# Attention and feed-forward on one core: unread products fill TensorE from its first microseconds

## The chip, the cores and the metric

The kernel runs on one core of a Trainium2 chip. The metric is the device time of one execution in microseconds (us); smaller is better.

## What is computed

Causal attention over 8 batches of 8 heads, 576 tokens and 64 features a head, with 16 extra keys and values ("beacon") that every token sees; its output goes through a feed-forward layer of 512 to 2048 to 512 with a squared rectifier. Cut to what matters:

```python
k_all = concatenate([beacon_k, k], axis=2); v_all = concatenate([beacon_v, v], axis=2)
scores = q @ k_all.T / sqrt(64)          # later tokens masked
a = exp(scores - max); a /= a.sum(-1)
x = (a @ v_all) as [4608 tokens, 512]
out = maximum(x @ w_in, 0) ** 2 @ w_out  # float32
```

## The kernel before, in words

A batch's heads are handled in four pairs. For each pair, q and k are turned so that features lie on partitions: batches 0 to 2 by transposes on TensorE (L635 where VectorE or ScalarE has first regrouped the data to full width, L638 straight from the cast data), later ones by DMA. VectorE and ScalarE copy the results to `kT` and `qT` (L437 and L439, which also hold all casts). Scores come from products that use 64 of the 128 rows of the array (L764), ScalarE takes the exponential into `pt` (L781), VectorE masks it (L799, L803), TensorE multiplies with the values `vb` (L819), VectorE normalises (L834, L835), and TensorE (batch 0, L883) or a DMA turns the result into `xT`. Batch 0 does this in two phases, tokens up to 240 first, so that the feed-forward part can start early. The feed-forward part goes by chunks of 512 tokens: products with `w_in` (L947), rectifier (L964, L966), square (L973), products with `w_out` (L987), copy and store.

Loads of q and k of the first batches, of some values and of the weights are issued by GpSimd (L599, L484, L908, L917), the others by SyncE. GpSimd also casts most values and makes the identity `ident` from a tile that VectorE has zeroed (L409).

The order of the instructions on every engine is made when the kernel is built. `Order.run` (L155) plays through the operations with a duration, a priority and dependences for each, an own model of the DMA rings, and pools of PSUM banks; each engine's queue is then emitted in the order found. That plan knows nothing of the chip's real times, and the queue of each engine is fixed by it.

The planner has a filler: where TensorE is free in the plan's time between the two values of `FILL` (L136) and no operation is ready, it puts in a pair of products of the identity with itself into the PSUM bank that has been free the longest. Nobody reads these. Their form follows the operation before: 64 rows (L533), 64 columns (L535) or the full array (L537). `mode` stands for that form; where it changes, the plan adds `DRAIN` to the duration. A filler counts 0.11 us in the plan. It takes the place in the queue that the plan gives it, however late the queue is on the chip.

Of the kernel before, what the change touches and what calls it, by code (L numbers as in the profile page):

```python
# [129 lines left out]
class Order:  # L130
# [2 lines left out]

    LAT = {"PE": 0.2, "ACT": 0.15, "DVE": 0.12, "POOL": 0.15, "SP": 0.1, "-": 0.0}
    DRAIN = 0.096
    FILL = (10.0, 22.0)  # L136
    filler = None
    START = {"PE": 0.0, "ACT": 0.0, "DVE": 1.5, "POOL": 0.5, "SP": 0.0, "-": 0.0}

# [15 lines left out]
    def run(self):  # L155
# [19 lines left out]
        full = False  # L175
# [5 lines left out]
        now = 0.0  # L181
        mode = None
        while events:
            now = events[0][0]
# [6 lines left out]
            full = full and rings.packets("SP") > rings.ROOM  # L191
            while events and events[0][0] <= now + 1e-9:
                _, _, kind, op = heapq.heappop(events)
# [17 lines left out]
            while again:  # L211
                again = False
                for e in engines:
                    if free[e] > now + 1e-9 or (e == "SP" and full):
                        continue
                    best = None
# [4 lines left out]
                    for op in avail[e]:  # L221
# [21 lines left out]
                        if best is None or op.prio < best.prio:  # L243
                            best = op
                    if best is None:
                        best = fallback
                    if best is None and e == "PE" and self.filler is not None and self.FILL[0] <= now < self.FILL[1]:
                        spot = self.pools["ps"].oldest()
                        if spot is not None:
                            best = self.filler(spot, mode or "full")  # L250
                            self.ops.append(best)
                            avail[e].append(best)
                    if best is None:
                        continue
                    op = best
# [13 lines left out]
                    if e == "PE":  # L269
                        dur += self.DRAIN * (mode not in (None, op.mode))  # L270
                        mode = op.mode
# [6 lines left out]
                    if op.dma:  # L278
                        rings.put(e, op, now + (0.75 + 0.6 * op.dma if e == "POOL" else 0.9))
                        under[e] += 1  # L280
                        full = full or (e == "SP" and rings.packets(e) > rings.ROOM)
# [29 lines left out]
def kernel(  # L311
# [11 lines left out]
    nc = tc.nc  # L323
# [17 lines left out]
    def sb(name, shape, dt):  # L341
        return pool.tile(shape, dt, name=name)
# [26 lines left out]
    ident = sb("ident", [128, 128], BF16)  # L369
    warm = sb("warm", [128, 8], FP32)  # L370
    xT = sb("xT", [128, NMC, RING], BF16)
# [4 lines left out]
    ps = psum.tile([128, 8, 512], FP32, name="ps")  # L376
# [25 lines left out]
    order.wait_for = wait_for  # L402
    add = order.add

    nc.vector.memset(warm, 0.0)
    for i in range(2):
        nc.vector.memset(kT[i][:, :, Nb + S:NT * 128], 0.0)
# [115 lines left out]
        deps += [o for p in range(HP * (b - 2), HP * (b - 1)) for o in qk_ops[p]]  # L523
        trans[b, x] = [add(f"tr{b}{x}", "SP", 3.8, emit, prio=prio, deps=deps, dma=3.4, margin=2.0)]

    def filler(spot, mode):


        def emit(e):
            for i in range(2):  # L530
                half = slice(64 * i, 64 * i + 64)
                if mode == "rows":
                    nc.tensor.matmul(ps[:, spot, 0:128], ident[0:64, :], ident[0:64, :], start=True, stop=True)  # L533
                elif mode == "columns":
                    nc.tensor.matmul(ps[half, spot, 0:128], ident[:, half], ident, start=True, stop=True)  # L535
                else:
                    nc.tensor.matmul(ps[:, spot, 0:128], ident, ident, start=True, stop=True)  # L537

        op = Op("fill", "PE", 0.11, emit, mode=mode)
        op.left, op.held = 0, None  # L540
        return op

# [600 lines left out]
```

## Time and profile before

| what | us |
|---|---|
| median of 3 runs | 339.43 |
| lowest and highest run | 338.14, 339.49 |
| profiled execution | 338.65 |
| its span, first to last instruction | 336.9 |
| TensorE busy in the span | 327.1 |

The profile is of one execution. Its span leaves out what lies around the instructions, 338.65 - 336.9 = 1.75 us. Times in the rows of the prediction count from the start of the span. PE is TensorE's products, PEld its weight loads, DVE VectorE, ACT ScalarE, POOL GpSimd, SP SyncE; a q behind the name is the engine's sequencer. A product's duration runs from its start to its modelled end, so neighbouring products overlap, and the time that one costs in a queue is the distance of the starts.

### The profile page before, as it was taken

Reading aid. Unit: us, or ns where it says so; the run is one execution under the profiler, and the core shown is the slowest. Engines: PE = TensorE matmul, PEld = TensorE weight load, DVE = VectorE, ACT = ScalarE, POOL = GpSimd, SP = SyncE. Lnnn points to the kernel's source line nnn. Section 1 sums busy time; section 2 is a strip of 40 time slices with the busy share of each in tenths; the row PEclk is TensorE's granted clock in tenths of the full one; section 3 lists DMA queues with packets and bytes.
Section 4 is the critical chain, followed back from the end, with each engine's and each line's share of the span. In section 5 each row is a group of like instructions: output and inputs, shape, how many; then the busy total and the mean of one; then the engine's idle time right before and its main releaser. Section 6 shows DMA issues by size and latency. Waiting matters only on the chain.

```text
span 336.9 us, 7692 instructions
## 1 busy us (share of the span) xinstructions
PE 327.1 (97%) x3172; PEld 184.2 (55%) x3172; DVE 160.5 (48%) x323; ACT 193.6 (57%) x300; POOL 86.8 (26%) x135
## 2 busy tenths in 40 slices
PE   3999999999999999999999999999999999999995
PEld 2778766545545555554468845545554544444444
DVE  6669977267604761475245632673246503301400
ACT  3887974597457647465656745755656226515611
POOL 7765911425122605140512351220000000000000
PEclk9999999999999999999999999999999999999999
DMA  9999999699959999799989996991310041011003
GB/s 167 196 207 210 206 203 207 147 247 179 221 104 223 241 199 176 185 208 228 206 121 257 242 210 138 209 196 32 104 62 2 14 120 63 0 62 64 0 17 110
DMA packets 138211, 50.38 MB, mean 150 GB/s; under 512 B 124176, under 2 KB 133264, under 8 KB 138176
## 3 DMA queue, kind: packets, MB, share of 16 engines
q1 hardware_dynamic: 128304, 40.42, 57.7%
q0 software_dynamic: 9520, 9.11, 16.3%
q8 instruction: 25, 0.41, 0.6%
q10 hardware_dynamic: 352, 0.36, 0.4%
q14 instruction: 10, 0.08, 0.1%
HBM read 37.22 MB, written 9.44 MB: 138 GB/s over the span
## 4 chain that ended last, share of the span: by engine, by line
PE 93%; DMA 2%; POOL 1%; DVE 1%; issue 1%; ACT 0%; POOLq 0%
PE ps L947 37%; PE ps L987 36%; PE ps L819 9%; PE ps L764 8%; DMA qk_area<-in_q_dram 2%; PE ps L635 1%; PE ps L1030 1%; POOL qk_area L599 1%; PE ps L883 1%; DVE g L966 0%; PE ps L537 0%; POOL vb L439 0%; PE ps L533 0%; POOL w_in L908 0%; DVE g L973 0%
## 5 line engine op out<-in xcount | busy, mean ns | idle before, releaser
L947 PE MATMUL ps<-xT,w_in 128*128 128x512 bf16 (+3 forms) x704 | 133.7, 340 | 0.2
L987 PE MATMUL ps<-w_out,g 128*128 128x512 bf16 x560 | 128.4, 379 | 0.0
L781 ACT ACTIVATE pt<-ps 128x1024 bf16<-128x1024 f32 (+3 forms) x128 | 102.9, 874 | 18.3 <-PE ps L764 18.1
L947 PEld LDWEIGHTS <-w_in 128*128 128x128 bf16 x704 | 65.9, 98 | 55.2 <-issue 3.9
L964 ACT ACTIVATE g<-ps 128x512 bf16<-128x512 f32 (+2 forms) x116 | 65.5, 568 | 39.1 <-PE ps L947 38.6
L987 PEld LDWEIGHTS <-g 128*128 128x128 bf16 x560 | 52.1, 98 | 61.1 <-issue 3.6
L973 DVE TENSOR_TENSOR g<-g 128x1024 bf16<-128x1024 bf16 (+2 forms) x80 | 52.1, 654 | 69.6 <-ACT g L964 69.4
L437 ACT COPY osb<-ps 128x512 f32<-128x512 f32 (+2 forms) x37 | 21.3, 576 | 68.8 <-PE ps L987 54.6
L439 POOL CAST qk_area<-stg 128x512 bf16<-128x512 f32 (+2 forms) x50 | 34.2, 688 | 67.5 <-DMA stg<-in_q_dram 41.0
L439 POOL CAST vb<-stg 128x512 bf16<-128x512 f32 (+1 forms) x39 | 26.1, 675 | 63.3 <-DMA stg<-in_v_dram 63.2
L799 DVE TENSOR_TENSOR pt<-pt,tri 128x1024 bf16<-128x1024 bf16 (+1 forms) x36 | 23.5, 654 | 34.2 <-ACT pt L781 34.2
L819 PEld LDWEIGHTS <-pt 128*128 128x128 bf16 (+1 forms) x960 | 34.2, 98 | 6.3 <-ACT pt L781 0.4
L966 DVE TENSOR_SCALAR g<-ps 128x512 bf16<-128x512 f32 (+2 forms) x44 | 26.8, 611 | 19.7 <-PE ps L947 19.4
L819 PE MATMUL ps<-vb,pt 128*128 128x65 bf16 (+1 forms) x960 | 35.6, 195 | 0.4 <-POOL vb L439 0.3
L764 PE MATMUL ps<-qT,kT 64*128 64x80 bf16 (+6 forms) x680 | 32.9, 235 | 0.0
L764 PEld LDWEIGHTS <-kT 64*128 64x128 bf16 x680 | 19.0, 96 | 16.8 <-issue 13.8
L835 DVE TENSOR_TENSOR xn<-ps,rcp 128x640 bf16<-128x640 f32 (+2 forms) x36 | 27.0, 750 | 1.8 <-DVE rcp L834 0.5
L834 DVE RECIPROCAL rcp<-ps 128x10 f32<-128x10 f32 (+2 forms) x36 | 7.5, 209 | 28.9 <-PE ps L819 28.9
L437 ACT COPY qT<-ps 128x576 bf16<-128x576 bf16 x12 | 7.6, 644 | 8.4 <-PE ps L635 7.4
L803 DVE TENSOR_TENSOR pt<-pt,tri 80x160 bf16<-80x160 bf16 x32 | 11.1, 347 | 0.0
L439 DVE COPY kT<-ps 128x576 bf16<-128x576 bf16 x12 | 8.9, 751 | 1.8 <-PE ps L638 1.2
L635 PE MATMUL ps<-ident,sparek 96*128 96x96 bf16 x18 | 1.5, 229 | 5.8 <-DVE sparek L439 5.8
(52 smaller groups left out, 80.4 us busy)
## 6 DMA issues: line engine op xcount, KB each, us to landing
out_dram<-osb SPq DMA_DIRECT2D x17, 512.0 KB, 3.6
stg<-in_v_dram SPq DMA_DIRECT2D x20, 256.0 KB, 5.1
stg<-in_q_dram SPq DMA_DIRECT2D x20, 256.0 KB, 5.5
stg<-in_k_dram SPq DMA_DIRECT2D x15, 256.0 KB, 4.3
w_in<-in_moe_w_in_dram POOLq DMA_DIRECT2D x4, 512.0 KB, 8.8
w_out<-in_moe_w_out_dram POOLq DMA_DIRECT2D x4, 512.0 KB, 11.6
stg<-in_v_dram SPq DMA_DIRECT2D x7, 224.0 KB, 4.5
qk_area<-in_k_dram POOLq DMA_DIRECT2D x4, 288.0 KB, 11.5
```

What stands on the lines that cost most here:

```text
L437: nc.scalar.copy(dst, src)
L439: eng[e].tensor_copy(dst, src)
L764: nc.tensor.matmul(st[:, hj, lo + col:lo + col + t1 - t0], kT[x.b % 2][hp, x.pr, 128 * c:128 * c + 128], qT[x.b % 2][hp, x.pr, t0:t1], sta ...
L781: nc.scalar.activation(pt[x.take_pt.held[0]][:, :, off:off + width], pair(box["qk"], k)[:, :, lo:lo + width], AF.Exp, bias=0.0, scale=scale)
L799: nc.vector.tensor_tensor(out=d, in0=d, in1=tri[:, m0:m0 + m, :][:, None].to_broadcast([128, 2, m, 128]), op=ALU.min)
L819: nc.tensor.matmul(a[:, hj, (t - tl[0]) * (D + 1):(t - tl[0] + 1) * (D + 1)], P[0:rr, hj, o:o + 128], vb[b % 2][0:rr, c, h, :], start=(c = ...
L835: nc.vector.tensor_tensor(out=xn[b % 2].rearrange("p t (h d) -> p h t d", d=D)[:, 2 * pr:2 * pr + 2, tl[0]:tl[0] + nt], in0=a[:, :, :, 0:D ...
L947: nc.tensor.matmul(h[:, lo - spans[0][0]:hi - spans[0][0]], w_in_sb[:, mc, ft * 128:(ft + 1) * 128], xT[:, mc, lo % RING:lo % RING + hi - lo],
L964: nc.scalar.activation(dst, h, AF.Relu, bias=0.0, scale=1.0)
L966: nc.vector.tensor_scalar(out=dst, in0=h, scalar1=0.0, scalar2=None, op0=ALU.max)
L973: nc.vector.tensor_tensor(out=d, in0=d, in1=d, op=ALU.mult)
L987: nc.tensor.matmul(o, G[:, fc, ts * 128:(ts + 1) * 128], w_out_sb[:, fc, :], start=(fc == 0), stop=(fc == NFT - 1))
```

## The change

The planner's fillers may come from 0.6 us of its time on, instead of 10.0. Up to 2.6 they are one product of 128x128 with 128x512 from a zeroed stretch of `xT`, called `hot`, into bank 7, and count 0.43 us. After that they are pairs of products of the identity, which count 0.22 us up to 6.0 and 0.11 us behind. The form with 64 rows is gone: after an operation of that form the filler is of the full array. After one of the 64-column form a pair still has that form, but the plan takes every filler as one of the full array, and adds `DRAIN` where the operation before had another form. VectorE zeroes `hot` as its first instruction.

```diff
-    FILL = (10.0, 22.0)
+    FILL = (0.6, 22.0)
...
-                            best = self.filler(spot, mode or "full")
+                            best = self.filler(spot, mode or "full", now)
...
+    hot = xT[:, 0, 0:512]
+    nc.vector.memset(hot, 0.0)
     nc.vector.memset(warm, 0.0)
...
-    def filler(spot, mode):
-
+    def filler(spot, mode, now):
+
+
+        mode = "columns" if mode == "columns" else "full"
+        if now < 2.6:
+            def emit(e):
+                nc.tensor.matmul(ps[:, 7, :], hot[:, 0:128], hot, start=True, stop=True)
+
+            op = Op("fill", "PE", 0.43, emit)
+            op.left, op.held = 0, None
+            return op
 
         def emit(e):
             for i in range(2):
                 half = slice(64 * i, 64 * i + 64)
-                if mode == "rows":
-                    nc.tensor.matmul(ps[:, spot, 0:128], ident[0:64, :], ident[0:64, :], start=True, stop=True)
-                elif mode == "columns":
+                if mode == "columns":
                     nc.tensor.matmul(ps[half, spot, 0:128], ident[:, half], ident, start=True, stop=True)
                 else:
                     nc.tensor.matmul(ps[:, spot, 0:128], ident, ident, start=True, stop=True)
 
-        op = Op("fill", "PE", 0.11, emit, mode=mode)
+        op = Op("fill", "PE", 0.22 if now < 6.0 else 0.11, emit, mode=mode)
```

## The prediction before the run

> **What bounds the kernel now.** I read the page first, then the instructions of TensorE in order of time, then the groups by shape, the waits and the single DMA issues. The page says who is the bound:
>
> ```profile
> span 336.9 us, 7692 instructions
> PE 327.1 (97%) x3172; PEld 184.2 (55%) x3172; DVE 160.5 (48%) x323; ACT 193.6 (57%) x300; POOL 86.8 (26%) x135
> PEclk9999999999999999999999999999999999999999
> ```
>
> TensorE is busy for all but 9.8 us of the span. So a change can win only at the start, where TensorE has nothing to do or is slow, or it must take work out of the queue behind. The clock row shows full speed from the first slice; the next rows show that it can't be trusted there. Start, duration, operation, count, and in brackets the idle time before:
>
> ```profile
> 5.80 0.66 PE L635 MATMUL ps<-ident,sparek 96*128 96x96 bf16 x6 [5.80 <-DVE sparek L439]
> ...
> 8.65 1.27 PE L638 MATMUL ps<-ident,qk_area 96*64 96x96 bf16 x24
> 9.86 0.84 PE L764 MATMUL ps<-qT,kT 64*128 64x240 bf16 x8
> 10.63 1.17 PE L638 MATMUL ps<-ident,qk_area 96*64 96x96 bf16 x24
> 11.73 1.53 PE L764 MATMUL ps<-qT,kT 64*128 64x240 bf16 x16
> 13.52 1.10 PE L819 MATMUL ps<-vb,pt 128*128 128x65 bf16 x12 [0.26 <-POOL vb L439]
> 14.75 0.38 PE L883 MATMUL ps<-ident,xn 112*128 112x112 bf16 x2
> 14.92 0.85 PE L537 MATMUL ps<-ident 128*128 128x128 bf16 x6
> 15.56 0.54 PE L819 MATMUL ps<-vb,pt 128*128 128x65 bf16 x6
> 15.91 0.62 PE L537 MATMUL ps<-ident 128*128 128x128 bf16 x4
> 16.32 0.40 PE L883 MATMUL ps<-ident,xn 112*128 112x112 bf16 x2
> 16.52 0.54 PE L819 MATMUL ps<-vb,pt 128*128 128x65 bf16 x6
> 16.99 0.53 PE L764 MATMUL ps<-qT,kT 64*128 64x336 bf16 x4
> 17.45 0.38 PE L883 MATMUL ps<-ident,xn 112*128 112x112 bf16 x2
> 17.76 0.38 PE L764 MATMUL ps<-qT,kT 64*128 64x208 bf16 x4
> 17.98 0.72 PE L533 MATMUL ps<-ident 64*128 64x128 bf16 x10
> 18.63 0.28 PE L883 MATMUL ps<-ident,xn 112*128 112x112 bf16 x2
> 18.85 0.35 PE L764 MATMUL ps<-qT,kT 64*128 64x336 bf16 x4
> 19.04 0.38 PE L533 MATMUL ps<-ident 64*128 64x128 bf16 x4
> 19.31 0.35 PE L764 MATMUL ps<-qT,kT 64*128 64x336 bf16 x4
> 19.59 0.99 PE L947 MATMUL ps<-xT,w_in 128*128 128x240 bf16 x8
> ```
>
> Compare like with like: two L883 take 0.38 to 0.40 us up to 17.45, and 0.28 at 18.63; four L764 of width 336 take 0.53 at 16.99 and 0.35 at 18.85. Six fillers of 128 columns take 0.85 us at 14.92, ten take 0.72 at 17.98. The groups by shape give single durations of a 128x128 product, the first from 13 to 16 us, the second from 18 to 20 us:
>
> ```profile
> L537 PE MATMUL ps<-ident 128*128 128x128 bf16 x7 | 1.1, 311 | 0.0
> ```
> ```profile
> L883 PE MATMUL ps<-ident,xn 128*128 128x128 bf16 x1 | 0.2, 222 | 0.0
> ```
>
> In a queue, a filler costs (850 - 311) / 5 = 108 ns at 14.92 and (720 - 222) / 9 = 55 ns at 17.98. So the array ran at half clock from its first product at 5.80 until about 17.8 us, and at full clock from there. It opened 3.0 us after the unbroken work from 14.75, but not in the 7.5 us from 5.80 to 13.26, which are transposes and 64-row products.
>
> From 14.75 on there is no idle time in brackets in these rows: TensorE is bound by its own queue, whose order is fixed when the kernel is built. The first useful product of the dense part, L947, comes at 19.59. Whatever lets that queue reach a given product earlier moves the end, until data that don't depend on TensorE come last. Two such gates stand in the trace:
>
> ```profile
> L908 POOL DMA_DIRECT2D w_in<-in_moe_w_in_dram x1: 772/772/772, 10.9 to 10.9; - x1
> DMA to landing us min/median/max: 7.2/7.2/7.2
> ```
> ```profile
> 10.93 0.77 POOL L908 DMA_DIRECT2D w_in<-in_moe_w_in_dram  x1 [3.56 <-DMA qk_area<-in_q_dram]
> ...
> 12.60 0.87 POOL L439 CAST vb<-stg 128x512 bf16<-128x512 f32 x1
> ...
> 39.90 1.33 POOL L439 CAST vb<-stg 128x512 bf16<-128x512 f32 x2
> ```
> ```profile
> 41.71 1.08 PE L819 MATMUL ps<-vb,pt 128*128 128x65 bf16 x30
> ```
>
> The first quarter of w_in lands at 10.93 + 7.2 = 18.13; its issue waited for a DMA, not for TensorE. The last values of batch 1 are cast by 39.90 + 1.33 = 41.23, and batch 1's first value products start at 41.71, 0.48 later. GpSimd's cast from 12.60 ends at 13.47 and releases the value products at 13.52, so handing over costs 0.05.
>
> **The change, part by part.** *Memset of `hot`.* 512 bf16 are 256 words per partition, the size of a row that is there:
>
> ```profile
> 1.57 0.27 DVE L410 MEMSET bks<- 128x256 uint32 x1
> ...
> 2.48 1.65 DVE L416 MEMSET pt<- 128x96 uint32 x12
> 2.85 0.30 POOL masks.py:199 TENSOR_SCALAR_AFFINE_SELECT ident<-ident 128x128 bf16<-128x128 bf16 x1
> ...
> 5.19 0.56 DVE L439 CAST sparek<-g 96x768 bf16<-96x768 f32 x1 [1.05 <-DMA g<-in_k_dram]
> ```
>
> It delays VectorE's memsets by 0.27 us, and they end at 4.40 instead of 4.13. The cast at 5.19 waits 1.05 us for a DMA, so this costs nothing; without that cover it would be 0.27.
>
> *Fillers ahead of the first transposes.* Five products of 512 columns at 4 x 108 = 0.43 us each are 2.2 us, from about 1.3 (after the memset) to 3.5; `ident` is ready at 3.15. The remaining 2.3 us up to 5.80 hold about 21 products of 128 columns at 108 ns. TensorE idles there now, so their price lies in how far they run past 5.80. The planner thinks in its own time, so I allow 0.0 to 0.4 us, and take 0.2. Behind them wait the transposes at 5.80, but the value products at 13.52 wait for GpSimd anyhow. So up to that gate the price is nothing, at most 0.4 if the transposes' lateness reached it.
>
> *What they buy.* They are 4.5 us of unbroken full-array products, more than the 3.0 us after which the array opened in the trace. I take it as open by 6 to 8 us.
>
> [...]
>
> With the clock open, products between 5.80 and 13.26 take about half the time, but three things there are not TensorE's: the arriving heads, the casts, and GpSimd's cast that ends at 13.47. So nothing is won before 13.52. From 14.75 to 17.76 it is: ten fillers at 108 - 55 = 53 ns less, 0.53; two groups of six value products at about 0.2 less, 0.4 (bounds 0.1 and 0.3 each, from the L883 pairs' 0.1 and the half of 0.54); three pairs of transposes at 0.1 less, 0.3; one group of four scores at 0.53 - 0.35 = 0.18. Together 1.4 us. Not all of it lies on the path, because a transpose waits for VectorE's normalisation:
>
> ```profile
> 17.41 0.17 DVE L834 RECIPROCAL rcp<-ps 128x4 f32<-128x4 f32 x1
> ...
> 17.61 0.42 DVE L835 TENSOR_TENSOR xn<-ps,rcp 128x256 bf16<-128x256 f32 x1
> ...
> 19.02 0.28 DVE L439 COPY xT<-ps 128x240 bf16<-128x240 bf16 x1 [0.79 <-PE ps L883]
> ```
>
> These 0.17 + 0.42 + 0.28 = 0.87 us of VectorE for each head pair don't get shorter. I take 1.0 of the 1.4 (bounds 0.5 and 1.4). L947 would start at 18.6; w_in's quarter is there at 18.13, so this gate is just open.
>
> *How much is kept.* At 41.71 the queue would come 1.0 early, but the values are cast at 41.23. If the whole group waits, 41.28 is the earliest, and 0.43 is kept. If only products of the last column tile wait, half a group later (0.54 of 1.08), 0.97 is possible. I take 0.7.
>
> *Fillers in idle spots, none in the 64-row form.* The 14 products of L533 become full-size, in two spots. A full product between 64-row ones changes the form twice. What a change costs is bounded by the weight loads of the scores:
>
> ```profile
> PEld L764 <- issue: 13.8, 37, 0.4
> ```
>
> 13.8 / 37 = 0.37 us of idle weight loader for each entry into that form, some of it covered by the product still running; so 0 to 0.37 a change. Two spots, taken at 0.05 each, are 0.1, already inside the rounding of 0.7. New spots between the transposes before 13.52 cost nothing while GpSimd is last.
>
> The sum: 338.65 (the profiled execution, of which 336.9 is span) - 0.7 = **337.95 us**. The profiled execution is 0.78 below the median of 339.43; runs from 338.14 to 339.49 fit an opening that falls at another point of the work in each run, and the new kernel should vary less.
>
> **The rivals.** *A. The late gate is not there.* The planner counts in its own time and may put batch 1's value products later, or the wait is by tile. Then the w_in gate decides: 19.59 - 18.13 - 0.1 = 1.35 kept, 337.3. For it: only 0.48 us separate cast and use, so a slight reordering passes it. Against it: GpSimd's time there follows DMAs.
>
> *B. The clock isn't held, or doesn't open.* After the fillers come 7 us of transposes and 64-row products, which in this trace didn't open it. If they count as idleness, it closes again, opens near 17.8 as now, and three added fillers at 108 ns behind 13.52 cost 0.3: 338.95. Against it: the full clock at later groups of the same kinds, and fillers in the spots between. [...]
>
> *C. Slower: form changes in the queue.* If full fillers fall between 64-row scores behind 14.75, each spot holds up the queue by two changes at 0.37 = 0.74 us, in which nothing else runs. The queue is 1.0 early at 18.6; four spots (the two of now and as many new ones) take 2.96, so it is 1.96 late and nothing gives that back: 338.65 + 1.96 = 340.6. It turns into a loss against the profiled execution from the second spot on (1.48 over 1.0). For it: two such spots stand at 17.98 and 19.04, with unbroken work behind. Against it: at 17.76, 18.63 and 18.85 the queue goes from scores to full products and back without idle time in brackets, so most of the 0.37 seems covered.
>
> **How the numbers follow.** The forecast has 0.42, A 0.25, B 0.18, C 0.15. About 0.5% (1.70 us of 339.43, so 337.73 and 341.13) is what a measurement can tell from no change. Faster by more: all of A and a quarter of the forecast, 0.35. Slower by more: the half of C with five spots or more, 0.08. Within: 0.57. The range goes from 336.8 (A, with half a microsecond less) to 340.2 (C with three spots is 338.65 + 2.22 - 1.0 = 339.9, and 0.3 of spread): about 0.07 is left out below and 0.10 above.
>
> **What would show it.** Products of L635 from about 5.8 us at shorter durations, a 128x128 filler at 222 ns ahead of 13.5: the clock. L947's first product near 18.6 instead of 19.59: the gain. An idle gap, or none, ahead of batch 1's L819 near 41.3 us: the late gate. Idle weight loads of L764 rising over 13.8: rival C. I am wrong if L883 still takes 0.38 near 16 us, if L947 starts early but the end doesn't follow by other waits than these, or if the order of the queue behind 20 us is another one.

## The result, and the profile after

| | before | after |
|---|---|---|
| median, us | 338.60 (19 runs, 336.95 to 341.79) | 340.89 (19 runs, 339.63 to 343.44) |
| profiled execution, us | 338.65 | 343.17 |
| its span, us | 336.9 | 341.5 |

The ratio is 1.0068, with a 95% interval from 1.0047 to 1.0088: the change makes the kernel slower by some 2.3 us. That lies above the range on record, which ended at 340.2. The profiled execution of after is near the top of its own spread, so its rows show 4.6 us of loss in span where the median has 2.3.

One sentence on the change above is wrong: the pair of fillers does pass its form on (`mode=mode` in the last line of the diff), so a filler with 64 columns would be planned as one; only the `hot` products always count as full array. In the plan of after no filler follows a 64-column operation, so the sentence changes no number.

The page of after:

```profile
span 341.5 us, 7750 instructions
PE 330.2 (97%) x3195; PEld 184.6 (54%) x3195; DVE 165.0 (48%) x326; ACT 193.9 (57%) x299; POOL 85.5 (25%) x134
PEclk9879999999999999999999999999999999999999
```

The clock row, full throughout for before, now has a dip in its second and third slice, 8.5 to 25.6 us. TensorE's instructions in order of time, after (start, duration, line, count, idle time before):

```profile
1.26 2.31 PE L534 MATMUL ps<-xT 128*128 128x512 bf16 x5 [1.26 <-DVE warm L407]
3.36 2.43 PE L546 MATMUL ps<-ident 128*128 128x128 bf16 x28
5.63 0.42 PE L644 MATMUL ps<-ident,sparek 96*128 96x96 bf16 x6
...
10.63 1.03 PE L773 MATMUL ps<-qT,kT 64*128 64x240 bf16 x12
13.46 0.33 PE L773 MATMUL ps<-qT,kT 64*128 64x240 bf16 x4 [1.80 <-DVE kT L441]
13.72 0.23 PE L828 MATMUL ps<-vb,pt 128*128 128x65 bf16 x2
14.13 0.28 PE L828 MATMUL ps<-vb,pt 128*128 128x65 bf16 x4 [0.17 <-DVE vb L441]
14.87 0.38 PE L828 MATMUL ps<-vb,pt 128*128 128x65 bf16 x6 [0.46 <-DVE pt L808]
15.76 0.38 PE L892 MATMUL ps<-ident,xn 112*128 112x112 bf16 x2 [0.51 <-DVE xn L844]
...
20.17 0.53 PE L773 MATMUL ps<-qT,kT 64*128 64x336 bf16 x4
20.62 0.61 PE L546 MATMUL ps<-ident 128*128 128x128 bf16 x4
21.03 1.01 PE L956 MATMUL ps<-xT,w_in 128*128 128x240 bf16 x4
```

The first five products with `hot` and 28 of the identity fill the start, and the first transposes run at 0.42 us for six where before took 0.66: the clock is open there. But TensorE then idles 1.80 us ahead of 13.46, the normalised heads come at 15.76 instead of 14.75, four scores of width 336 again take 0.53 at 20.17, and the first product with `w_in` starts at 21.03 instead of 19.59. Of these 1.44 us, 15.76 - 14.75 = 1.01 are there before the dense part begins; the remaining 0.43 come between 15.76 and 21.03, at half clock. These are figures of one execution. Two kernels below with the same TensorE queue and the clock open at this place, early_hold and early_hold_cast_act, differ by 19.27 - 18.07 = 1.20 us at this product, so single executions carry a spread of that size.

The first cause stands in VectorE's queue, after and then before, and in GpSimd's of after:

```profile
8.90 0.42 DVE L808 TENSOR_TENSOR pt<-pt,tri 128x512 bf16<-128x512 bf16 x1
12.31 0.43 DVE L441 CAST vb<-stg 128x512 bf16<-128x512 f32 x1 [2.99 <-DMA stg<-in_v_dram]
12.65 0.75 DVE L441 COPY kT<-ps 128x576 bf16<-128x576 bf16 x1
13.32 0.76 DVE L441 CAST vb<-stg 128x512 bf16<-128x512 f32 x1
13.99 1.16 DVE L808 TENSOR_TENSOR pt<-pt,tri 128x512 bf16<-128x512 bf16 x2
```
```profile
11.33 0.42 DVE L799 TENSOR_TENSOR pt<-pt,tri 128x512 bf16<-128x512 bf16 x1 [0.85 <-ACT pt L781]
11.67 0.75 DVE L439 COPY kT<-ps 128x576 bf16<-128x576 bf16 x1
12.57 0.43 DVE L439 CAST vb<-stg 128x512 bf16<-128x512 f32 x1
```
```profile
11.26 1.80 POOL L486 DMA_DIRECT2D stg<-in_v_dram  x2
13.05 2.26 POOL L917 DMA_DIRECT2D w_in<-in_moe_w_in_dram  x3
```

In before, VectorE masks, copies the fourth pair's `kT`, then casts the second tile of values; the first tile is GpSimd's, the cast at 12.60 in the prediction's rows. In after GpSimd has no cast between its loads of values and of `w_in`: the first tile's cast has moved to VectorE, ahead of that copy. It waits 2.99 us for its load, and TensorE waits for the copy. The order comes from the plan: there the last early filler begins at 5.610 and counts 0.22, so the first transposes stand at 5.830 instead of 5.734. This 0.096 us makes the second mask ready at 10.601 where it was ready at 10.505. VectorE is idle in the plan from 10.301, and at 10.560 the load of the first tile lands there. In before the mask had VectorE by then and the cast went to GpSimd; in after the mask comes too late by 0.041 us, and VectorE takes the cast.

The second cause is the clock. The trace's clock record for after says open from 4.83, closed from 15.07, open again from 21.90; for before, open from 17.82. These stretches are whole multiples of 3.413 us (10.24 is three, 6.83 is two), as they are in every profile below in which the clock closes again; the shortest, in slip_alone, is 3.41. Busy time by windows of that length, after (PE, PEld, DVE, ACT, POOL busy, granted clock, DMA):

```profile
4.83:8.25 3.42, 3.08 (x73) 2.57 (x70) 2.66 (x6) 2.25 (x4) 2.26 (x7) 1.00 1.28 187
8.25:11.66 3.41, 2.53 (x56) 1.66 (x56) 1.07 (x2) 3.04 (x6) 1.17 (x2) 1.00 1.22 232
11.66:15.07 3.41, 0.98 (x16) 0.62 (x16) 2.76 (x5) 2.05 (x4) 3.41 (x5) 1.00 1.13 170
15.07:18.49 3.42, 2.91 (x35) 1.69 (x32) 3.27 (x13) 2.36 (x4) 2.79 (x6) 0.50 1.15 237
18.49:21.90 3.41, 3.41 (x28) 1.96 (x26) 1.09 (x5) 2.67 (x3) 2.71 (x5) 0.50 1.24 205
21.90:25.31 3.41, 3.41 (x59) 2.38 (x59) 2.31 (x8) 2.87 (x4) 1.07 (x2) 1.00 1.27 204
```

The window with only 0.98 us of busy TensorE is followed by the half clock, and it takes two windows of the dense part to open it again. So the cold stretch, which in before lay over thin work from 5.80 to 17.82, lies over denser work from 15.07 to 21.90.

A third thing shows further on. TensorE, after:

```profile
41.48 0.62 PE L956 MATMUL ps<-xT,w_in 128*128 128x272 bf16 x4 [1.73 <-DVE g L975]
...
45.03 1.08 PE L828 MATMUL ps<-vb,pt 128*128 128x65 bf16 x30
```

It waits 1.73 us for VectorE, and batch 1's value products start at 45.03 instead of 41.71. Shortly before, VectorE had a square that in before takes 0.43 (the mean of eight):

```profile
38.62 1.78 DVE L982 TENSOR_TENSOR g<-g 128x544 bf16<-128x544 bf16 x1
41.00 0.42 DVE L975 TENSOR_SCALAR g<-ps 128x272 bf16<-128x272 f32 x1
```

The rectifier at 41.00, for which TensorE waits, stands behind it in VectorE's queue, with one copy of 0.74 between them.

### The profile page after: what moved, and what is told of

Same layout as the page of the kernel before. It is cut to its first block, busy times and chain, and to the rows that moved or that the text cites. A ratio compares the mean times of both kernels' runs of the same rounds, so it can differ in the third digit from the quotient of the medians.

```text
span 341.5 us, 7750 instructions
## 1 busy us (share of the span) xinstructions
PE 330.2 (97%) x3195; PEld 184.6 (54%) x3195; DVE 165.0 (48%) x326; ACT 193.9 (57%) x299; POOL 85.5 (25%) x134
## 4 chain that ended last, share of the span: by engine, by line
PE 91%; DVE 4%; DMA 3%; issue 1%; ACT 1%; POOL 0%; SPq 0%; DVEq 0%; POOLq 0%
PE ps L996 36%; PE ps L956 36%; PE ps L828 8%; PE ps L773 8%; DMA stg<-in_v_dram 2%; DMA qk_area<-in_q_dram 1%; DVE g L982 1%; PE ps L1039 1%; PE ps L644 1%; DVE pt L808 1%; DVE kT L441 1%; DVE qk_area L441 1%; PE ps L892 1%; PE ps L546 1%; DVE g L975 0%
## 5 line engine op out<-in xcount | busy, mean ns | idle before, releaser
L982 DVE TENSOR_TENSOR g<-g 128x1024 bf16<-128x1024 bf16 (+2 forms) x80 | 54.6, 685 | 68.0 <-ACT g L973 67.3
L441 POOL CAST vb<-stg 128x512 bf16<-128x512 f32 (+1 forms) x38 | 25.1, 668 | 62.3 <-DMA stg<-in_v_dram 53.5
L975 DVE TENSOR_SCALAR g<-ps 128x512 bf16<-128x512 f32 (+2 forms) x45 | 27.5, 613 | 21.3 <-PE ps L956 20.7
L773 PEld LDWEIGHTS <-kT 64*128 64x128 bf16 x680 | 18.6, 95 | 19.7 <-issue 16.1
L812 DVE TENSOR_TENSOR pt<-pt,tri 80x160 bf16<-80x160 bf16 x32 | 10.3, 321 | 0.0
L486 POOL DMA_DIRECT2D stg<-in_v_dram x7 | 6.0, 866 | 4.9 <-DMA w_in<-in_moe_w_in_dram 4.0
```

The source lines that it names most:

```text
L441: eng[e].tensor_copy(dst, src)
L773: nc.tensor.matmul(st[:, hj, lo + col:lo + col + t1 - t0], kT[x.b % 2][hp, x.pr, 128 * c:128 * c + 128], qT[x.b % 2][hp, x.pr, t0:t1], sta ...
L975: nc.vector.tensor_scalar(out=dst, in0=h, scalar1=0.0, scalar2=None, op0=ALU.max)
L982: nc.vector.tensor_tensor(out=d, in0=d, in1=d, op=ALU.mult)
```

## The experiments

Theory: the early fillers win at the start, but shift the plan, and the clock that they open closes again in the stretch that waits for data. Rivals: the forms (C of the prediction) cost the time; the shifted order alone does; or a lead at the start is worth nothing. "Ratio" is against before, run beside it on the same chip, with its interval. "First w_in" is the start of the first product with `w_in` in the profile (19.59 in before). All added products are unread, and no run leaves out needed work.

| run | clock, us | first w_in | ratio | median |
|---|---|---|---|---|
| forms_alone | open from 12.83 | 18.31 | 1.0003 (0.9981 to 1.0025) | 338.54 |
| early_in_order | open 5.52 to 12.34, from 19.17 | 19.99 | 1.0037 (1.0018 to 1.0055) | 340.06 |
| early_in_order_rows_kept | open 4.25 to 14.49, from 17.91 | 18.95 | 1.0062 (1.0033 to 1.0091) | 340.21 |
| slip_alone | open 12.58 to 15.99, from 26.24 | 21.06 | 1.0120 (1.0085 to 1.0156) | 343.28 |
| after_rows_kept | open 5.90 to 12.73, from 22.97 | 20.80 | 1.0122 (1.0088 to 1.0156) | 342.89 |
| slip_forms | open from 22.37 | 20.22 | 1.0023 (0.9999 to 1.0048) | 339.30 |
| no_fill | open from 21.61 | 18.77 | 1.0034 (1.0010 to 1.0058) | 339.98 |
| early_then_delay | open 4.76 to 15.00, from 21.83 | 21.19 | 1.0047 (1.0019 to 1.0076) | 340.50 |
| early_hold | open from 4.02 | 19.27 | 1.0016 (0.9994 to 1.0038) | 339.39 |
| after_hold | open from 5.87 | 19.44 | 1.0044 (1.0024 to 1.0064) | 339.83 |
| slip_hold | open from 14.29 | 21.30 | 1.0120 (1.0087 to 1.0153) | 343.14 |
| slip_early_hold | open from 4.05 | 19.02 | 1.0048 (1.0023 to 1.0073) | 340.20 |
| early_hold_cast_act | open from 5.43 | 18.07 | 1.0008 (0.9989 to 1.0027) | 338.73 |
| before_cast_act | open from 22.62 | 20.86 | 1.0008 (0.9983 to 1.0033) | 339.26 |

The clock and the first w_in are of one execution each; the ratios are over 6 to 12 executions of the run. How far one execution can lie from another shows in before_cast_act: up to the first w_in its TensorE queue is that of before, and yet it comes there at 20.86 with the clock closed up to 22.62. In forms_alone and early_in_order four scores that stand ahead of the first product with `w_in` elsewhere stand behind it, which flatters their figure by some 0.3 us.

**The forms.** The changed kernel without its early fillers:

```diff
-    FILL = (0.6, 22.0)
+    FILL = (10.0, 22.0)
...
-    hot = xT[:, 0, 0:512]
-    nc.vector.memset(hot, 0.0)
```

> The kernel before with nothing but the filler's form: in idle spots after 64-row scores a full-size pair instead of the 64-row pair; no early filler, window from 10.0 us of the plan. The plan then orders a few rectifiers and squares otherwise. Theories P and K: within 0.998 to 1.003. Theory F: slower by 1.0 to 2.3 us, ratio 1.003 to 1.007, with idle weight loads ahead of the scores above the 13.8 us of the kernel before.

Measured 1.0003. The idle weight loader ahead of the scores, forms_alone:

```profile
PEld L771 <- issue: 14.8, 40, 0.4
```

14.8 us in 40 entries against 13.8 in 37: three more form changes, and no time that shows. Rival C falls. This run also bears on what a lead is worth, below.

**The early fillers in an unchanged order.** Two kernels in which no filler stands between 5.5 and 10.0 of the plan. early_in_order_rows_kept also keeps the 64-row form, and every engine's queue of needed work is that of before; early_in_order has the new forms, and its queues are those of forms_alone.

```diff
-e == "PE" and self.filler is not None and self.FILL[0] <= now < self.FILL[1]:
+e == "PE" and self.filler is not None and (0.6 <= now < 5.5 or 10.0 <= now < 22.0):
```

> The early fillers alone: none starts between 5.5 and 10.0 us of the plan, and idle spots keep the 64-row form, so that every engine's queue of real work is that of the kernel before, in the same order. Theory P (the plan): the loss came from the last early filler, which ends 0.096 us late in the plan and lets VectorE take the cast of v's first tile ahead of a copy that TensorE needs. Then this kernel is not slower than before: ratio 0.996 to 1.001, first product with w_in (L947 before) at 18.3 to 19.6 us. Theory K (the clock): the early opening is followed by a closing near 15 us, as in the changed kernel's clock (open 4.83 to 15.07 us, closed to 21.90), which puts the slow stretch over denser work than before. Then it is slower by 1.0 to 2.3 us, ratio 1.003 to 1.007, with durations of 311 ns for a 128x128 product after 15 us.

> The changed kernel without the slip alone: no early filler starts between 5.5 and 10.0 us of the plan, so that the first transposes and VectorE's queue up to the rectifiers stand as before; early fillers and full-size form stay. Its order of real work is that of the run with the forms alone (1.0003). Theory P (only the slip costs): 0.997 to 1.002. Theory K (the early opening is followed by a closing near 14 to 15 us): about the early fillers' own ratio, 1.003 to 1.009. Theory L (the queue's lead at 19 us is lost near 38 to 42 us, where VectorE's copies and squares take 1.8 us instead of 0.4 beside GpSimd's casts and DMA issues, and more than the lead is lost): the same, 1.003 to 1.009, with such a long VectorE row.

Measured 1.0062 and 1.0037: early fillers cost time with no shift of the order at all. In both profiles the clock closes. early_in_order_rows_kept, by windows:

```profile
7.67:11.08 3.41, 2.57 (x66) 1.81 (x68) 2.13 (x5) 3.18 (x6) 0.76 (x1) 1.00 1.30 233
11.08:14.49 3.41, 1.83 (x30) 1.34 (x30) 2.23 (x8) 3.39 (x5) 3.41 (x6) 1.00 1.20 183
14.49:17.91 3.42, 3.42 (x41) 2.73 (x37) 2.77 (x9) 1.89 (x3) 2.84 (x6) 0.50 1.16 240
17.91:21.32 3.41, 3.41 (x48) 2.19 (x47) 1.90 (x6) 2.88 (x6) 3.32 (x6) 1.00 1.24 207
```

It reopens at 17.91, about where before opened, so this execution is still 0.64 ahead at its first `w_in` product (18.95), and yet ends at 339.55 against 338.65. So in this execution it isn't the clock that takes the lead. It goes at 39 us; TensorE, VectorE and GpSimd of the same kernel:

```profile
18.95 0.99 PE L957 MATMUL ps<-xT,w_in 128*128 128x240 bf16 x8
...
39.24 0.43 PE L645 MATMUL ps<-ident,qk_area 96*128 96x96 bf16 x6 [0.96 <-DVE qk_area L441]
```
```profile
37.41 1.77 DVE L441 COPY qk_area<-qk_area 96x768 bf16<-96x768 bf16 x1
```
```profile
37.11 0.69 POOL L609 DMA_DIRECT2D qk_area<-in_k_dram  x1
37.79 1.18 POOL L441 CAST vb<-stg 128x512 bf16<-128x512 f32 x2
```

The copy takes 1.77 us while GpSimd issues a transfer and casts; TensorE waits 0.96 for it. The six copies of this shape, first in this kernel and then in before (min/median/max):

```profile
L441 DVE COPY qk_area<-qk_area x6: 346/358/1772, 29.9 to 37.4; 96x768 bf16<-96x768 bf16 x6
```
```profile
L439 DVE COPY qk_area<-qk_area x6: 342/348/1015, 30.9 to 37.4; 96x768 bf16<-96x768 bf16 x6
```

GpSimd's work beside it may be what stretches the copy. The rows fit that in part: in before, the copy of 0.35 at 36.15 runs into GpSimd's cast at 36.24, and there the cast is the longer one, 0.73 where the median of before's 39 casts of values is 0.62. No run here shows the cause.

**The shifted order alone.** The kernel before, told that TensorE begins at 5.83 of the plan:

```diff
-    START = {"PE": 0.0, "ACT": 0.0, ...
+    START = {"PE": 5.83, "ACT": 0.0, ...
```

> The kernel before with nothing but the plan's slip: TensorE counts as free from 5.83 us of the plan instead of 0, so that the first transposes stand at 5.830 as in the changed plan instead of 5.734. No early filler, 64-row fillers kept. VectorE's queue then has the cast of v's first tile ahead of the copy of the fourth k, as in the changed kernel. Theory P: as slow as the changed kernel or nearly, ratio 1.004 to 1.009, an idle spot of TensorE of 0.5 to 1.8 us before batch 0's last first-phase scores, near 13.4 us. Theory K: no early opening, so no closing at 15 us; the stall is there but the ratio is 0.998 to 1.003.

after_rows_kept is the changed kernel with the 64-row form put back; its needed work has the order of slip_alone.

> The changed kernel with the 64-row form of the filler put back: early fillers and slip stay; its order of real work is that of the run with the slip alone. Theory P: the slip decides, ratio 1.004 to 1.009, like the run with the slip alone. Theory K: 1.004 to 1.009 too, because early fillers and stall are both there; the two differ in the run with the slip alone. Theory F (full fillers between 64-row scores change the form and hold up the queue): most of the loss goes, ratio 0.997 to 1.002.

slip_forms is slip_alone with the changed kernel's forms, which is exactly the changed kernel's order without an early filler.

> The kernel before with the slip and the full-size fillers, no early filler: every engine's queue of real work is exactly the changed kernel's. If the order alone makes the loss: 1.004 to 1.012. If the early fillers make it: 0.999 to 1.003. The changed kernel has 1.0068, the same order with the clock held 1.0044, so I expect 1.004 to 1.009, with a clock that opens at 12 to 20 us and, where it opens before 14, closes again in the stall.

slip_alone (1.0120) and after_rows_kept (1.0122) came out above every range that was expected of them; slip_forms (1.0023) missed its 1.004 to 1.009 and fell where the early fillers would make the loss. With 64-row fillers the shifted order costs 1.2%, with or without early fillers; with the changed kernel's own forms 0.2%, an interval that reaches no change. TensorE of slip_alone shows the wait for `kT` with no early filler in the queue:

```profile
11.60 1.17 PE L764 MATMUL ps<-qT,kT 64*128 64x240 bf16 x12
13.55 0.33 PE L764 MATMUL ps<-qT,kT 64*128 64x240 bf16 x4 [0.79 <-DVE kT L439]
...
21.06 0.98 PE L947 MATMUL ps<-xT,w_in 128*128 128x240 bf16 x4
```

So the shifted order costs time without any early filler. It isn't told apart from the clock here, which in this profile closes at 15.99 and opens again only at 26.24. Its price varies: VectorE's cast, which waits for the load of values, starts at 12.31 in after, 12.02 in slip_alone, 11.51 in slip_forms and 11.08 in slip_hold, and in slip_forms TensorE didn't wait for `kT` at all. The two shifted orders, with and without 64-row fillers, also differ further on: in the one with them SyncE has a load of batch 3's q ahead of batch 1's transposes into `xT`, which neither before nor after has. No run tests what that costs. By their middles, the whole change (1.0047 to 1.0088) against slip_forms (0.9999 to 1.0048) would put most of the loss on the early fillers; the two intervals overlap by a hair, so this is likely, not shown.

**Is it the clock?** Unread products are to keep it open. In early_hold, on early_in_order_rows_kept, 4, 14 and 10 products of the identity go ahead of three operations of the thin stretch; after_hold does so to the changed kernel, slip_hold and slip_early_hold to slip_alone and after_rows_kept, with 30, 8 and 10.

```diff
+    extra = {"qk3.0.0": 4, "av0.0": 14, "xtp0.0.0": 10}
...
+                if op.name in self.extra:
+                    self.more(op, self.extra[op.name])
                 op.insts = op.emit(e)
...
+    def more(op, n):
+        for _ in range(n):
+            nc.tensor.matmul(ps[:, op.held[0], 0:128], ident, ident, start=True, stop=True)
```

> The early fillers alone, in the order of before, with 28 more unread 128x128 products in the three spots where TensorE sat idle between 11.4 and 14 us (4, 14 and 10, 1.5 us in all). Theory K: the clock stays open from about 4.5 us on (a 128x128 product takes 222 ns at 15 us), and the ratio to before falls to 0.996 to 1.002. Theory L: the clock stays open, the lead at the first product with w_in is 0.6 to 1.3 us, but it is lost near 38 to 42 us all the same; ratio 1.002 to 1.008.

> The changed kernel with 48 more unread 128x128 products where TensorE sat idle: 30 before batch 0's last first-phase scores (1.65 us at 55 ns, idle was 1.80), 8 before the second pair's value products, 10 before the first transposes of the output. The slip and its order stay. Theory K: the clock stays open through 15 to 22 us, the first product with w_in comes at 19.0 to 20.0 us instead of 21.03, and the ratio to before is 0.999 to 1.004. Theory P (the order costs by its waits, whatever the clock): 1.005 to 1.009.

> Early fillers, the slip, 64-row fillers kept (1.0122 without more), and 48 more unread 128x128 products in the idle spots from 11 to 16 us, as in after_hold. Its order of real work is that of slip_alone. With the early fillers the 30 products run at full clock, 1.65 us, in an idle spot of 1 to 1.8 us. Theory K: the clock stays open from 4 to 6 us on, and the ratio falls to 1.002 to 1.007. Theory P: the clock stays open and the ratio stays at 1.008 to 1.013, with TensorE waits for VectorE and ScalarE between 30 and 60 us.

> The slip alone (1.012) with 48 more unread 128x128 products in its idle spots from 11 to 16 us, no early filler. Theory K: most of the 1.012 is the clock, which closed at 15.99 and stayed closed to 26.24; with the added products the clock opens by 13 to 16 us and stays open, the first product with w_in comes at 19.0 to 20.2 us instead of 21.06, and the ratio falls to 1.001 to 1.006. Theory P (the waits of the order cost by themselves): 1.008 to 1.014.

The clock stayed open in the profiles of the first three. early_in_order_rows_kept's 1.0062 went to 1.0016 in early_hold, after_rows_kept's 1.0122 to 1.0048 in slip_early_hold, and after's 1.0068 to 1.0044 in after_hold. Only the second pair of intervals lies apart; the first overlaps by 0.0005, the last by more, and 1.0044 lies between what the two theories had for it. In slip_early_hold, 48 more products that nobody reads made the kernel shorter by 0.7%, with the same order of needed work. The clock, which its profile shows open, is the likely reason; that the added products also move the later work against the transfers isn't excluded. In the first pair the two profiled executions end alike, at 339.55 and 339.54, so there the gain lies in executions that were not profiled.

slip_hold, at 1.0120, could not tell what it was made for. Without early fillers its 30 products ran mostly at half clock (it opened at 14.29) and held the queue for 15.27 - 12.79 = 2.48 us, in a place where slip_alone idles 0.79:

```profile
12.79 2.55 PE L551 MATMUL ps<-ident 128*128 128x128 bf16 x30
15.27 0.33 PE L774 MATMUL ps<-qT,kT 64*128 64x240 bf16 x4
```

**How thin is too thin?** I worked out, for each window of 3.413 us counted from the changes in the clock record, the share of the array's time that the products starting in it stream: for each product columns x rows used x columns used / (128 x 128) / speed, summed. The speed is an estimate, 2.4 or 1.2 columns a ns by the granted clock: products of 512 columns with `w_out` in before follow each other every 216 ns at full clock (the median; 2.37), and three of the four distances between the products with `hot` in after, at half clock, are 426 or 427 ns (1.20). For the window of after that closed the clock, the rows by shape are two scores of 240 and two of 128 columns on half the array and twelve value products of 65: (736 / 2 + 780) / 2.4 = 478 ns of 3413, 0.14. The 22 openings and six closings at the start of the 16 profiles, and the windows nearest to them in share that changed nothing:

```
half clock, opened after shares of       0.77 0.78 0.79 0.82 0.84 0.84 0.84 0.84 0.84 0.84 0.85 0.86 0.86 0.90 0.91 0.91 0.91 0.94 0.94 1.00 1.00 1.00
half clock, stayed so after shares up to 0.74 0.74 0.75 0.77 0.79
open, closed after shares of             0.14 0.25 0.25 0.29 0.33 0.36
open, stayed so after shares from        0.41 0.41 0.43 0.45 0.45 0.45 0.46 0.46
```

Further on, the window of after from 38.97, with the wait of 1.73 us in it, had 0.39 and left the clock open.

no_fill, before without any filler (`FILL = (1e9, 1e9)`), was a forecast by this table:

> The kernel before without any filler. It shows what the opening of the clock by the old fillers in idle spots is worth. By the windows of 3.41 us read from the clock of the eight runs, a closed clock opened behind windows in which the array's streaming (columns by rows used, over the time) was 0.77 or more, and stayed closed at 0.74 or less. Without the 24 fillers the window from about 14.5 us has 0.5 to 0.7 of it, so the clock opens one window later, at 20 to 25 us: ratio 1.002 to 1.010. If the fillers are worth nothing: 0.998 to 1.002.

Its clock opened at 21.61; the share in its window from 14.78 was 0.64 where before's from 14.41, with its 12 pairs of fillers, was 0.82. It cost 0.34%: the old fillers earn their place. Its first product with `w_in` came earlier than in before (18.77), since nothing unread stood in front, and the half clock behind took that back.

The changes in one profile lie on a grid of 3.413 us, whose place differs from run to run (the first opening is at 17.82 in before and at 4.83 in after, 12.99 apart, which is 3.81 windows); and the clock closed behind a window that products fill to 0.36. Transposes are counted in these shares. Without them, windows of 0.50 (slip_alone from 9.17) and 0.55 (forms_alone from 9.42) opened the clock and one of 0.66 (slip_forms from 15.54) did not; counted by area, transposes included, they are 0.79, 0.84 and 0.77. Even so counted, one of 0.79 (before_cast_act from 8.97) stayed closed.

**Is a lead worth anything?** early_then_delay puts 12 products ahead of the first product with `w_in` in early_in_order_rows_kept (`extra = {"s1.0.0.0": 12}`).

> The early fillers alone, in the order of before, with 12 more unread 128x128 products (0.66 us at 55 ns) set right before the first product with w_in: they use up the lead of 0.64 us that the early fillers alone had there, so that everything behind stands at the time of before. Theory L (the lead itself runs into GpSimd's casts near 38 us): it is no slower than the early fillers alone in spite of the added work, ratio to before 0.998 to 1.003, no TensorE wait for VectorE's copy of qk_area near 39 us. Theory K (the closing of the clock costs): the added work comes on top, ratio 1.006 to 1.010.

Measured 1.0047, profile 340.81. In its profile the clock was closed up to 21.83, so that there was no lead to take away: it decides nothing. forms_alone says more. Its second four products with `w_in`, which have the same needed work ahead of them as in before, start at 19.10 where those of before start at 20.02, a lead of 0.92 us. Batch 1's value products then start at 41.51 instead of 41.71, and from 133 us on its value products are 0.19 late. No early filler and no closing of the clock is in it, and the lead still comes to nothing.

**Where a lead goes.** early_hold_cast_act takes batch 1's last three casts of values from GpSimd to ScalarE, in early_hold; before_cast_act does it in before.

```diff
-copy_on(e, vb...
+copy_on("ACT" if b == 1 and c >= 2 else e, vb...
```

> The early fillers with the 28 products that hold the clock (1.0016), and batch 1's last three casts of v on ScalarE as in the run beside it. Theory L: no VectorE copy or square of over 1 us between 34 and 42 us, the lead of 0.3 to 1.3 us at the first product with w_in is still there at batch 1's first value products, and the ratio is 0.3 to 0.4% below that of early_hold: 0.996 to 0.999. Theory D (the arrival of the loads sets the pace at 36 to 42 us, whoever casts): same as early_hold, 1.000 to 1.004.

> The kernel before with batch 1's last three casts of v on ScalarE instead of GpSimd, at the place in the queues that the plan gives them; a control for the next run. Theory L (VectorE's copies near 38 us are held up by GpSimd's casts and DMA issues, and that is what a lead runs into): without a lead there is little to win, ratio 0.997 to 1.002. If ScalarE then waits for the loads in its queue, 1.002 to 1.006.

TensorE, early_hold_cast_act:

```profile
18.07 0.99 PE L967 MATMUL ps<-xT,w_in 128*128 128x240 bf16 x8
...
39.81 1.09 PE L967 MATMUL ps<-xT,w_in 128*128 128x272 bf16 x8 [0.44 <-ACT g L984]
...
40.74 1.09 PE L839 MATMUL ps<-vb,pt 128*128 128x65 bf16 x30
```

Here the lead is 19.59 - 18.07 = 1.52 us at the first `w_in` product and still 41.71 - 40.74 = 0.97 at batch 1's values, while early_hold was 0.43 late there. Most of that difference isn't the moved casts': 1.20 of it is there at the first `w_in` product, before any of them runs. Between the two places this run loses 0.55 and early_hold 0.75. Neither has an instruction of VectorE over 1 us between 30 and 46; what is left is a wait of 0.44 for ScalarE at 39.81, where early_hold waited 0.34 and 0.27 for VectorE. So the moved casts are worth some 0.2 us, and another engine takes the rest. Behind, value products are 1.2 ahead at 56 us, 0.8 at 74 and 0.35 from 125 on. The ratio of 1.0008 missed the 0.996 to 0.999 that the theory of the casts had; the median of 338.73 can't be told from before's, nor from that of before_cast_act. No run beat before.

## Why the prediction was wrong, point by point

- *Memset.* Right: VectorE still waits for a DMA behind it, 0.54 us ahead of the first cast.
- *Price of the early fillers, 0.0 to 0.4, covered by the gate at 13.52.* Failed. I looked for their price in the queue of TensorE, where the first transposes stand at 5.63, not late at all. The price lies in the plan: 0.096 us of shift gives VectorE the cast on which the prediction's gate at 13.52 stood as GpSimd's, and puts it ahead of a copy that TensorE needs. The gate moved to VectorE, and the wait there is 1.80 us. The prediction named "the order of the queue behind 20 us" as a risk; it was VectorE's, behind 10.
- *The clock opens by 6 to 8 us.* Right, and sooner: 4.83. The last fillers ahead of 5.63 take 0.22 us each.
- *What it buys: 1.0 us at the first product with `w_in`.* This step failed, and with it the forecast. It took an open clock as lasting, where the trace has it closed from 15.07 to 21.90 and the product at 21.03 instead of 18.6. With the clock held open the product came at 19.27 and 18.07 in two kernels with the order of before, 0.32 and 1.52 ahead, so the 1.0 is of the right size while the clock lasts. Rival B had the closing, but put the reopening "near 17.8 as now" and so got 338.95; in after it came at 21.90: the window from 15.07 was filled to 0.67 and left the clock at half, the one from 18.49 to 0.84, and behind it the clock opened. The filler's mean duration by shape from 13 to 16 us (the last number but one, in ns), in after and then in early_hold, where the clock was held:

```profile
L546 PE MATMUL ps<-ident 128*128 128x128 bf16 x1 | 0.3, 314 | 0.0
```
```profile
L551 PE MATMUL ps<-ident 128*128 128x128 bf16 x6 | 0.5, 219 | 0.0
```

- *What is kept past the late gate: 0.7 us.* Failed too, and would have with the clock open: with it held and the order kept the ratio is 1.0016, not 0.998. The gate at 41.28 isn't what takes the lead, and it isn't fixed: in early_in_order_rows_kept batch 1's casts end at 38.34 + 0.62 = 38.96 instead of 41.23. The lead goes in waits at 39 to 40 us, for VectorE and, with the casts moved, for ScalarE, and behind 56 us. Rival A, in which the gate is absent, was right about the gate (value products at 40.74, and at 40.94 in slip_early_hold with the casts on GpSimd), and wrong that this is worth 1.35 (its own sum gives 1.36).
- *Forms.* Right in size: nothing measurable, with a ratio of 1.0003 and idle entries of the weight loader up from 37 to 40.
- The chance of 0.08 for slower by over 0.5% rested on forms alone. No case held that a clock which opens early and closes again can stay closed longer (here to 21.90 instead of 17.82), and over denser work, than one that never opened early, though B's condition was in the text.

What stays open: how the loss of the whole change splits between order and clock (after_hold keeps 0.44% with the clock open, slip_forms has 0.23% without early fillers; their intervals overlap); why the shifted order costs 1.2% with 64-row fillers and 0.2% without (SyncE's order is one untested candidate); what takes the lead back between 56 and 74 and between 74 and 125 us; and why shares of 0.77 to 0.79 open the clock in some runs and not in others. The clock was seen in one execution of each run; that the others differ by where the grid falls is inferred, not shown.

## What to carry to other kernels

Opening the clock ahead of work that waits for data didn't last here: at full clock a filler takes 55 ns of the queue instead of 108, so by that estimate the same data-bound work fills half the share of a window. Keep the stretch between filled to about half, as the held runs did (0.45 and more), or warm up only where dense work begins, which no run here tried; and look at the clock record after, not only at the first durations. Where a planner writes the queues, a filler isn't free because its engine is idle: compare every engine's order before and after. And before counting a lead as time, follow it along the path up to the end.

## What was not expected of the hardware

- In six profiles the clock closed, each time behind a window of 3.413 us with products for 0.14 to 0.36 of the array's time; the least filled window found that left it open had 0.39 (after, from 38.97). At half clock it opened behind windows of 0.77 to 1.00 and stayed as it was behind some of up to 0.79. The longest idle gap of TensorE in such a closing window was 0.55 us in early_in_order and 1.80 in after.
- Adding unread work went with a shorter kernel: 48 products of 128x128, of which 30 take 1.83 us at full clock, turned 1.0122 into 1.0048.
- A VectorE copy of 96x768 in bf16 took 0.35 us at the median of six in before and 0.36 in early_in_order_rows_kept, and there once 1.77, where GpSimd issued a transfer and cast; in after a square of 128x544 took 1.78 instead of before's 0.43 in such a stretch. Not every copy beside a cast is stretched: the one at 36.15 in before was not, and the cast was.
